# A fused attention and two feed-forward blocks: the position bias as one fp32 product per group, the second block on f16 pairs

## Chip, cores, metric

One core of a Trainium2 chip runs the whole kernel in one launch. The metric is the device time of one execution in microseconds. The kernel before took 663.27 us as the median of 3 runs (662.59 to 666.99).

## What is computed

For 2 batches of 8 heads, 576 positions and 64 features, the reference forms attention scores `0.125 * q k^T` and adds a position bias from a small network:

```
x    = log1p(|i - j|) / log1p(max(i, 1))
h    = max(x * w1 + b1, 0)          # 32 units
bias = h @ w2                       # 8 heads
```

A softmax over j follows, a product with v, then a first feed-forward block on 1152 tokens of 512 features (2048 hidden units, a rational function P(h)/Q(h) as activation), and a second one of the same size with `max(0.01 h, h)`. The weights of both blocks arrive as 64-bit floats. The result has to be good to about fp32, so every large product is split into a leading and a trailing part and made as three products: lead*lead, lead*trail, trail*lead.

## The kernel before, in words

The program is written out by hand, engine by engine, in this order.

**Bias stage.** The 576 query rows are handled in 36 groups of 16 rows (`NG`), four rows beside each other in four slots, each slot with 32 partitions for the 32 units. For each slot `b_mask` writes a 0/1 (VectorE) or sign (ScalarE) mask in f16: is the unit on for this distance? `MASKS` says which engine makes which of the four. `b_mm` makes two sums from these masks on TensorE, with f16 coefficients in two parts: per group 2 x 16 products, each with 32 output columns in one of the four column strips of the array. `b_t0` (ScalarE) scales the first sum by a row's factor, `b_t1` (GpSimd) multiplies by the table `te` of log distances, `b_out` (VectorE) adds the second sum, and a DMA on SP's queue puts the 128 x 576 result into the bias tiles. `BIAS_PLAN` says how many groups ahead each step is issued; `EXTRA` mixes in the loads and preparations of the first attention unit.

**Attention.** Eight units (a pair of heads, a batch) of nine tiles each: scores in three fp32r products (`qk`), bias added and minimum taken on VectorE (`ttr`), exp on ScalarE, split into f16 pairs, transposed by DMA, product with v in f16 (`av`). Then `xhi`/`xlo` split the result for the first block. `TAIL` and `START` mix in the beginning of the first block.

**First block.** 16 slices f of 128 hidden units. `w_load` fetches two halves of weights, `w_dve` turns 64-bit floats into fp32 on VectorE in three steps, `w_hi`/`w_lo` split them into fp32r pairs (ScalarE, GpSimd). `gemm1` makes 36 products of 384 columns a slice, the `r_...` steps compute the activation, `split_hi`/`split_lo` split it, `g2_mm` makes the second product over blocks of slices and `g2_acc` adds it up in SBUF. The order is that of a list scheduler (`arrange`) over these steps with assumed costs (`COST`) and ranks (`SHIFT`). For slices in `E_DVE`, which the scheduler does not know, `r_q1` is left out and `r_e` runs on VectorE in its place.

**Second block.** The same with `l_001`, `l_max` for the activation. The order is a fixed step plan (`PLAN2`); `g2_tok` makes 48 products of 512 columns a token tile over all slices and adds six blocks up in SBUF (`BLOCKS`). All its products are fp32r, on the same pairs of tiles as in the first block.

Of the kernel before, what the change touches and what calls it, by code (L numbers as in the profile page):

```python
# [26 lines left out]
MASKS = ('AVAA', 'VVAV', 'VVVV', 'VVAA')  # L27
BIAS_PLAN = [(3, 'mask', 2), (-1, 'mm', 1), (5, 'mask', 0), (1, 'mm', 0), (1, 'extra'), (-1, 'out'),
             (1, 't0'), (1, 't1'), (3, 'mask', 1), (3, 'mask', 3)]
O_LAG = (0, 1)  # L30
O_STEP = (3, 0)
G2_LAG = 10
# [8 lines left out]
}  # L41
E_DVE_1 = ()

SHIFT = {'g2_acc': 285.2,
         'g2_mm': 1.9,
         'g2_out': 44.7,
         'gemm1': 50.3,
         'r_abs': 71.3,
         'r_e': -48.0,
         'r_exp': 178.1,  # L50
         'r_fin': 2.1,
         'r_h2': -90.6,
         'r_h3': -51.4,
         'r_ln': -196.5,
         'r_q1': 110.6,
         'r_qa': -99.6,
         'r_qq': 49.4,
         'r_s1': 54.7,
         'r_v': 204.8,
         'split_hi': 156.3,  # L60
         'split_lo': 25.5,
         'w_dve0': 46.3,
         'w_dve1': 282.1,
         'w_dve2': 149.1,
         'w_hi': 297.1,
         'w_lo': 17.0,
         'w_load': -193.4}
SLACK = 0.34


def arrange(tasks, ends, free):
# [18 lines left out]
    rank = {k: way[k] + SHIFT[k[0]] for k in tasks}  # L90
# [3 lines left out]
    while todo:  # L94
# [7 lines left out]
        t, k = max(((t, k) for t, k in best[eng] if t <= first[eng] + SLACK), key=lambda x: rank[x[1]])  # L102
# [7 lines left out]
        for u in users[k]:  # L110
            missing[u] -= 1
            if not missing[u]:
                ready[u] = max(ends.get(x, 0.0) for x in tasks[u][2]) + 0.15
# [4 lines left out]
PLAN2 = [  # L118
    (6, "w_lo", 0),
    (5, "w_hi", 0),  # L120
    (4, "w_dve", 1),
    (5, "w_hi", 1),
    (7, "w_lo", 1),
    (-2, "gemm1", 3),
    (6, "split_hi"),
    (2, "l_max"),
    (4, "w_dve", 2),
    (3, "w_dve", 0),
    (5, "w_load"),
    (-3, "gemm1", 1),  # L130
    (-4, "gemm1", 0),
    (0, "l_001"),
    (-3, "gemm1", 2),
    (7, "split_lo", ()),
]
# [4 lines left out]
NEX = 2  # L140
HI_MERGED = ()
# [3 lines left out]
PAR = 168 + S // 4 + NG + len(MASKS)  # L145
# [41 lines left out]
E_DVE = (0, 1, 2)  # L187
XLO_POOL = False
EXTRA = [(2, 'load', 0), (4, 'load', 1), (22, 'load', 2), (33, 'load', 3), (35, 'v_scale', 1),
         (15, 'prep_ql', 0, 0), (4, 'late_constants'), (32, 'v_sum', 1), (29, 'prep_vd', 0),  # L190
         (20, 'prep_ql', 0, 1), (15, 'v_scale', 0), (11, 'prep_q', 0, 0), (16, 'prep_q', 0, 1),
         (8, 'v_sum', 0), (10, 'prep_k', 0), (28, 'prep_v8', 0)]
# [10 lines left out]
def host_constants():  # L203
# [5 lines left out]
    e = p // H  # L209

    def away(off):
        return np.abs(c[None, :] - S - off[:, None])

    dist = away(4 * g).astype(np.float16)
    tabs = psi[np.minimum(away(4 * e), S - 1)].astype(np.float32)
    first = np.array([first_row(n) for n in range(NG)])
    first_z = (first[:, None] + 16 * np.arange(4)[None, :]).reshape(-1)
    rows_z = psi_i[4 * g[:, None] + first_z[None, :]]
    rows_e = np.float32(1.0) / psi_i[4 * e[:, None] + first[None, :]]
# [3 lines left out]
    picks = np.array([[pat[y] == "A" for pat in MASKS] for y in range(4)]).repeat(32, 0)  # L223
    rows = np.concatenate([rows_z, rows_e, picks], 1).astype(np.float32)
    small = np.concatenate([eye, k == m[None, :]], 1).astype(np.float32)
    return rows, {
        "dist": np.ascontiguousarray(dist),
# [6 lines left out]
def attn_bias_moe_kernel(  # L234
# [8 lines left out]
    dist: bass.AP,  # L243
# [18 lines left out]
    ln15 = const.tile([128, 1], F32, name="ln15")  # L262

# [8 lines left out]
    ys = [pair_slot(2, p) for p in range(NP)]  # L272

# [7 lines left out]
    raw = const.tile([128, 2, DM], F32, name="raw")  # L281
# [5 lines left out]
    for m, t0 in (("1", 0), ("2", NF + 3)):  # L287
        for f in range(NF):
            if m == "2" or f > 2:
                w_pair.setdefault(t0 + f - 3, []).append(("i" + m, f))  # L290
            if m == "2" or f > 0:
                w_pair.setdefault(t0 + f + O_LAG[int(m) - 1] - (f < O_STEP[int(m) - 1]), []).append(("o" + m, f))
# [8 lines left out]
    def w_dve(t, k, x0=0, x1=2):  # L301
# [4 lines left out]
        for x in range(xs.start, xs.stop):  # L306
            assert holds["w64", x] == t
            holds["raw", x] = t
        if not wide:
            if k == 0:  # L310
                V.tensor_copy(raw[:, xs], w64[:, xs])
            return
        w = w64[:, xs].rearrange("p x (n y) -> p x n y", y=2)
        bits = raw[:, xs].bitcast(I32)
# [7 lines left out]

    def w_hi(t, x):
        if x < len(w_pair.get(t, ())):
            m, f = w_pair[t][x]
            ring = wi_ring if m[0] == "i" else wo_ring
            slot = ring[(f + NF * (m[1] == "2")) % len(ring)]
            assert holds["raw", x] == t
            holds[m[0], (f + NF * (m[1] == "2")) % len(ring)] = None
            w_got[m, f] = slot  # L330
            A.activation(w_got[m, f][0], raw[:, x], AF.Copy)  # L331

    def w_lo(t, x):
        if x < len(w_pair.get(t, ())):
            assert holds["raw", x] == t
            m, f = w_pair[t][x]
            holds[m[0], (f + NF * (m[1] == "2")) % len(wi_ring if m[0] == "i" else wo_ring)] = (m, f)
            hi_, lo_ = w_got[m, f]
            G.tensor_tensor(lo_, raw[:, x], hi_.bitcast(F32), ALU.subtract)  # L339

    def weights(m, f):
        ring = wi_ring if m[0] == "i" else wo_ring
        assert holds[m[0], (f + NF * (m[1] == "2")) % len(ring)] == (m, f), (m, f, holds)
        return w_got[m, f]
# [4 lines left out]
    def gemm1(m, f, kk, cs=range(3)):  # L349
        if kk == 0 and 0 in cs:  # L350
            hps[f] = psh[f % 2].tile([128, 3, 512], F32, tag="h", name="ph")
        ps = hps[f]
# [5 lines left out]
        for n, c in todo:  # L358
            w, x = ((hi_, xh), (hi_, xl), (lo_, xh))[n]
# [80 lines left out]
    def l_001(f):  # L440
        s1[f] = t32("s1", 3)
        A.activation(c3(s1[f]), hp(f, None), AF.Copy, scale=0.01)  # L442

    def l_max(f):
        V.tensor_tensor(c3(s1[f]), hp(f, None), c3(s1[f]), ALU.max)
# [6 lines left out]
    def split_lo(f, dve, c=None):  # L452
# [3 lines left out]

    early = {
        f.__name__: f
        for f in (r_abs, r_s1, r_qq, r_qa, r_h2, r_h3, r_ln, r_exp, r_q1, r_e, r_v, r_fin, split_hi, split_lo)
        + (w_load, w_dve, w_hi, w_lo)  # L460
# [67 lines left out]
    with ExitStack() as st:  # L528
# [8 lines left out]
        z = b1p.tile([128, 2 * S], F16, name="z")  # L537
# [4 lines left out]
        A.dma_start(out=z, in_=dist)  # L542
        SP.dma_start(out=te[:, halves[0]], in_=tabs[:, halves[0]])
# [3 lines left out]
        c0, c1 = 134 + S // 4, 134 + S // 4 + NG  # L547
        rows_z, rows_e, picks = pr[:, 134:c0], pr[:, c0:c1], pr[:, c1:]
# [10 lines left out]
        G.memset(ones, 1.0)  # L559
        G.memset(tiny, 1e-30)  # L560
        G.memset(ln15, float(15 * np.log(2)))

        sg, aw, rate = col1("sg"), col1("aw"), col1("rate")
        V.tensor_scalar(sg, wc[:, 0:1], 0.0, 2.0, ALU.is_ge, ALU.mult)
        V.tensor_scalar(sg, sg, -1.0, None, ALU.add)
        V.tensor_scalar(aw, wc[:, 0:1], sg, 1e-30, ALU.mult, ALU.max)
        V.reciprocal(aw, aw)
        V.tensor_tensor(rate, sg, wc[:, 1:2], ALU.mult)
        V.scalar_tensor_tensor(rate, rate, -1.0, aw, ALU.mult, ALU.mult)
        V.tensor_scalar(rate, rate, 13.2, -13.2, ALU.min, ALU.max)  # L570
        nwc = b1p.tile([128, 2], F32, name="nwc")
# [634 lines left out]
```

## Time and profile before

| | |
|---|---|
| median of 3 runs | 663.27 us (662.59 to 666.99) |
| the profiled execution | 666.41 us |
| its span, first to last instruction | 664.6 us |
| mean granted TensorE clock | 0.964 |
| busy: PE / DVE / ACT / POOL | 593.9 / 514.6 / 408.7 / 360.5 us |
| chain that ended last | PE 54%, DVE 18%, DMA 6%, ACT 5%, issue 5% |

PE is TensorE's product row, PEld its weight loads, DVE VectorE, ACT ScalarE, POOL GpSimd, SP the engine whose queue issues DMAs. `L360` is line 360 of the kernel. In a row of the grouped view, after the bar stand the busy time in us, the mean ns of one, and the idle time of that engine just before such instructions with what ended it. Products are pipelined, and their ends are modelled: a row of n products in a row shows n steps and one drain.

### The profile page before, as it was taken

To read this page: it belongs to the slowest core of one execution; us is meant where nothing else is said; L and a number is where in the kernel's file an instruction comes from. 1 tells how busy PE (TensorE), PEld (TensorE's weight loads), DVE (VectorE), ACT (ScalarE), POOL (GpSimd) and SP (SyncE) were. 2 spreads that over 40 slices of the span, in tenths; PEclk is the share of its full clock that TensorE was granted. 3 is DMA by queue.
4 is the path that set the end of the run, shared out by engine and by line. 5 is a ranking of instruction groups with operands and counts; after the bars stand their busy time and mean duration, and the time that the engine had idled before them with its cause. 6 is when DMAs were issued, how large, how long until landed. Compare 5 with 4: busy or idle time off the path is not lost.

```text
span 664.6 us, 11791 instructions
## 1 busy us (share of the span) xinstructions
PE 593.9 (89%) x4595; PEld 527.5 (79%) x4595; DVE 514.6 (77%) x788; ACT 408.7 (61%) x625; POOL 360.5 (54%) x263
## 2 busy tenths in 40 slices
PE   5767878898988857779999999999999999999998
PEld 3334557777777746779999999999999999999876
DVE  7999897979889787998999999997355745545463
ACT  9999678778878467687776786653355322322210
POOL 5766685757776512357567577652265443453340
PEclk9998979988989998879999999999999999999999
DMA  5767889999979912111131130121133221220113
GB/s 188 194 153 208 218 153 194 199 204 193 159 140 167 229 64 95 65 64 64 64 122 70 64 126 33 65 65 63 64 127 126 97 95 63 88 104 32 64 47 127
DMA packets 102199, 77.35 MB, mean 116 GB/s; under 512 B 86400, under 2 KB 86784, under 8 KB 102144
## 3 DMA queue, kind: packets, MB, share of 16 engines
q1 hardware_dynamic: 100848, 68.97, 40.7%
q10 hardware_dynamic: 1296, 7.64, 3.6%
q8 instruction: 36, 0.59, 0.4%
q14 instruction: 19, 0.16, 0.1%
HBM read 42.39 MB, written 2.36 MB: 67 GB/s over the span
## 4 chain that ended last, share of the span: by engine, by line
PE 54%; DVE 18%; DMA 6%; ACT 5%; issue 5%; POOL 2%; SPq 0%; DVEq 0%; POOLq 0%; ACTq 0%
PE ph L360 21%; PE pz L982 13%; PE py L941 11%; PE ps L722 5%; DMA biasr<-in_moe_w_in 3%; DVE raw L319 3%; DVE raw L317 2%; PE pv L814 2%; DVE raw L321 2%; DMA et<-hl 2%; ACT ex L750 1%; DVE pt L734 1%; DMA qkv<-in_qkv 1%; PE pr L841 1%; DVE ph L413 1%
## 5 line engine op out<-in xcount | busy, mean ns | idle before, releaser
L360 PE MATMUL ph<-bias,bias 128*128 128x384 f32 x1152 | 215.9, 341 | 14.6 <-DVE s L434 11.8
L360 PEld LDWEIGHTS ph<-bias,bias 128*128 128x128 f32 x1152 | 206.5, 192 | 20.3 <-ACT bias L951 6.9
L787 POOL TENSOR_TENSOR hl<-ex,hl 128x512 f16<-128x512 f32 (+2 forms) x94 | 92.3, 1000 | 35.2 <-DVE hl L774 18.8
L722 PE MATMUL ps<-kt,qz 128*128 128x288 f32 x432 | 81.0, 331 | 18.8 <-DVE mn L734 14.8
L339 POOL TENSOR_TENSOR wo<-raw,wo 128x512 fp32r<-128x512 f32 x23 | 31.1, 1351 | 116.8 <-ACT wo L331 116.8
L455 POOL TENSOR_TENSOR gl<-s,gh 128x1152 fp32r<-128x1152 f32 (+1 forms) x33 | 84.1, 2548 | 11.5 <-ACT gh L450 11.0
L722 PEld LDWEIGHTS ps<-kt,qz 128*128 128x128 f32 x432 | 65.5, 206 | 30.1 <-DVE mn L734 16.9
L339 POOL TENSOR_TENSOR bias<-raw,bias 128x512 fp32r<-128x512 f32 x37 | 51.1, 1382 | 58.7 <-ACT bias L331 48.5
L941 PE MATMUL py<-gh,wo 128*128 128x384 f32 x288 | 78.7, 337 | 1.7 <-DVE bias L953 1.6
L982 PE MATMUL pz<-wo,gh 128*128 128x512 f32 (+1 forms) x240 | 74.5, 386 | 0.3 <-DVE bias L990 0.3
L990 DVE TENSOR_TENSOR bias<-pz,bias 128x512 f32<-128x512 f32 x40 | 27.6, 690 | 52.9 <-PE pz L982 52.9
L750 ACT ACTIVATE ex<-pt,mn 128x576 f32<-128x576 f32 x72 | 55.2, 767 | 17.6 <-DVE mn L734 13.7
L630 PEld LDWEIGHTS <-coef 128*32 128x32 f16 x1152 | 28.5, 100 | 40.5 <-issue 25.8
L648 POOL TENSOR_TENSOR t<-t,te 128x576 f32<-128x576 f32 x36 | 47.0, 1311 | 22.4 <-DVE bb L653 12.7
L941 PEld LDWEIGHTS py<-gh,wo 128*128 128x128 f32 x288 | 52.5, 188 | 3.7 <-DVE bias L953 3.6
L442 ACT ACTIVATE s<-ph 128x1152 f32<-128x1152 f32 x16 | 18.2, 1136 | 57.9 <-PE ph L360 57.9
L734 DVE CUSTOM_DVE_ANT_0 pt<-ps,bias 128x576 f32<-128x576 f32 x64 | 47.5, 745 | 7.4 <-PE ps L722 5.3
L317 DVE TENSOR_SCALAR raw<-biasr 128x1024 int32<-128x1024 int32 (+1 forms) x40 | 33.6, 841 | 24.0 <-DMA biasr<-in_moe_w_in 22.6
L941 PE MATMUL py<-gl,wo 128*128 128x384 f32 x156 | 52.2, 334 | 0.0
L331 ACT ACTIVATE wo<-raw 128x512 fp32r<-128x512 f32 x27 | 16.9, 628 | 55.9 <-DVE raw L321 55.9
L982 PEld LDWEIGHTS pz<-wo,gh 128*128 128x128 f32 x240 | 44.3, 188 | 7.7 <-DVE bias L990 0.7
L982 PE MATMUL pz<-wo,gl 128*128 128x512 f32 (+1 forms) x129 | 50.1, 389 | 0.0
(134 smaller groups left out, 1185.5 us busy)
## 6 DMA issues: line engine op xcount, KB each, us to landing
biasr<-in_moe_w_in SPq DMA_DIRECT2D x32, 512.0 KB, 4.5
biasr<-in_moe_w_out SPq DMA_DIRECT2D x32, 512.0 KB, 3.6
bias<-bb SPq DMA_DIRECT2D x32, 288.0 KB, 3.9
qkv<-in_qkv ACTq DMA_DIRECT2D x8, 896.0 KB, 5.5
out<-bias SPq DMA_DIRECT2D x8, 256.0 KB, 2.0
biasr<-bb SPq DMA_DIRECT2D x8, 144.0 KB, 3.6
et<-hl SPq DMA_TRANSPOSE x40, 4.8
sm<-in_small SPq DMA_DIRECT2D x1, 416.0 KB, 5.1
```

The lines of the kernel that those rows point to most:

```text
L317: V.tensor_scalar(bits, hi32, 3, 0x3FFFFFF8, ALU.logical_shift_left, ALU.bitwise_and)
L339: G.tensor_tensor(lo_, raw[:, x], hi_.bitcast(F32), ALU.subtract)
L360: PE.matmul(ps[:, c, 0:CH], w[:, sl], x[kk][:, c * CH:(c + 1) * CH], start=(kk == 0 and n == 0), stop=(kk == KD - 1 and n == 2),)
L455: eng.tensor_tensor(part(gl, c), part(s1[f], c), part(gh, c).bitcast(F32), ALU.subtract)
L630: PE.matmul(ps[32 * c:32 * c + 32, lo:hi], coef[:, int(MASKS[n % len(MASKS)][c] == "A"), j, part], masks[n, c][:, lo // 64:hi // 64], star ...
L648: G.tensor_tensor(t1, t0s.pop(n), te[:, S - first_row(n):2 * S - first_row(n)], ALU.mult)
L722: PE.matmul(ps[:, c, 0:288], lt[:, a], kts[i][:, b, 288 * c:288 * c + 288], start=(n == 0), stop=(n == 2),)
L734: V.tensor_tensor_reduce(out=c2(pt), in0=s_ps.pop((i, j))[:, :, 0:288], in1=c2(bsrc), op0=ALU.add, op1=ALU.min, scale=1.0, scalar=3.0e38, ...
L750: A.activation(et, pt, AF.Exp, bias=mn, scale=-1.0, accum_out=sums[i][:, col:col + 1],)
L787: engines[j in at].tensor_tensor(hl[:, xs, dst], e9[:, xs, src], hl[:, xs, src], ALU.subtract)
L941: PE.matmul(ps[:, 0:CH], w[:, sl], gts[f][x][:, cs], start=(f == f0 and m == 0), stop=(f == f0 + nf - 1 and m == 2),)
L982: PE.matmul(ps[:, half], gts[f][x][:, sl], w[:, half], start=(f == f0 and m == 0), stop=(f == f0 + nf - 1 and m == 2),)
```

## The change

Bias: the unit's value itself is made in fp32, `max(slope * te, -b1)` on VectorE or `Relu(slope * te + b1)` on ScalarE, with `slope = w1 / log1p(i)` per row; one fp32 product with w2 per slot and half row sums the units; one ScalarE step negates it, adds a constant for the slots made on VectorE, and is the group's result. The masks, thresholds, coefficient splits, the multiplication by the table on GpSimd and the second sum go.

Second block: weights (per pair of halves) and tokens (per chunk of 384) are scaled by 2^15 over the root of their sum of squares and split into f16 pairs instead of fp32r pairs; products are f16; the scale is taken back when the second product is added up. New steps: `w_sq`, `w_sum`, `w_sig`, `w_lo2` per weight pair, `y_sq`, `x_sum`, `x_sig`, `x_cast`, `x_low`, `x_inv` per token chunk. Both halves of a load are now of one kind (two of w_in or two of w_out). The second product runs in eight blocks of two slices. The scheduler now orders both blocks in one list, with ranks that differ at the ends (`seam`), and there are two `raw` buffers. `E_DVE` is (0,) instead of (0, 1, 2).

```diff
-MASKS = ('AVAA', 'VVAV', 'VVVV', 'VVAA')
+MASKS = ('VAAV', 'AAVV', 'VVVV', 'VVVV')
+OUTS = 'AAAA'
-E_DVE = (0, 1, 2)
+E_DVE = (0,)
+BLOCKS_2 = [2] * 8
...
+    def w_sq(t):
+        if t in w_pair:
...
+                A.activation(junk, raws[max(t, 0) % 2], AF.Square, accum_out=w_ss[t])
+    def total(ss, col):
+        spare = live[-2][:, 0, 384 + col:385 + col]
+        for x in range(ss.shape[-1]):
+            PE.matmul(spare, ones_r, ss[:, x:x + 1], start=(x == 0), stop=(x == ss.shape[-1] - 1))
+        return spare
+    def root_of(dst, spare):
+        A.activation(dst, spare, AF.Ln, bias=tiny)
+        A.activation(dst, dst, AF.Exp, bias=ln15, scale=-0.5)
...
-            G.tensor_tensor(lo_, raw[:, x], hi_.bitcast(F32), ALU.subtract)
+                V.scalar_tensor_tensor(lo_, raws[max(t, 0) % 2][:, x], sig[m, f - f % 2][0], hi_, ALU.mult, ALU.subtract)
...
         def b_mask(n, c):
-            mk = mp.tile([128, 9, 66], F16, tag="mk", name="mk")[:, :, 0:64]
+            mk = mp.tile([128, S], F32, tag="mk", name="mk")
...
-                V.tensor_scalar(mk, zs, thr[:, col:col + 1], None, ALU.is_gt)
+                eng.tensor_scalar(mk, src, slope[:, col], off, ALU.mult, ALU.max)
...
+        def b_mm(n):
+            ps = (psa, psb)[n % 2].tile([128, 1024], F32, tag="AB"[n % 2], name="ps" + "AB"[n % 2])
+            for x in range(2):
+                for c in range(4):
+                    PE.matmul(
+                        ps[32 * c:32 * c + 32, 512 * x:512 * x + 288], wflat, masks[n, c][:, 288 * x:288 * x + 288],
+                        start=True, stop=True,
+                    )
...
-            V.scalar_tensor_tensor(bb, psB.pop(n)[:, 0:S], cab[:, v, 1:2], t1s.pop(n), ALU.add, ALU.add)
+                A.activation(to, ps[:, :, 0:288], AF.Identity, bias=base[:, v:v + 1], scale=-1.0)
...
-                V.tensor_tensor(dst, ps[:, half], dst, ALU.add)
+                V.scalar_tensor_tensor(dst, ps[:, part], back, dst, ALU.mult, ALU.add)
...
+        elif k[0][:4] == "gemm" and k[2] == 0 and (k[0] != "gemm2" or k[1] > 1):
+            for x in list(waiting):
+                ops[x[0]](x[1])
+                del waiting[x]
```

The last lines issue a pair's `w_sig` (which reads the sum from a spare column of the previous slice's PSUM tile) at the latest before the next slice's first product, which writes that tile.

## Rows read from the trace of the kernel before

**Rows 1.** Stretch, length, busy us of PE, PEld, DVE, ACT, POOL; PE clock, DMA share, GB/s.

```profile
0.00:79.00 79.00, 54.97 (x1180) 31.90 (x1180) 72.10 (x150) 71.55 (x109) 51.83 (x50) 0.98 0.68 191
...
245.00:300.00 55.00, 39.24 (x181) 37.72 (x182) 49.59 (x45) 39.36 (x46) 21.09 (x12) 0.81 0.20 69
300.00:460.00 160.00, 158.26 (x905) 156.13 (x904) 150.09 (x180) 111.74 (x128) 99.44 (x51) 1.00 0.21 73
460.00:640.00 180.00, 179.28 (x915) 164.03 (x914) 93.80 (x103) 57.02 (x71) 79.24 (x45) 1.00 0.24 85
```

**Rows 2.** What PE waited for, 245 to 300 us: total, times, longest in us.

```profile
PE ph L360 <- DVE s L434: 11.8, 3, 6.6
```

**Rows 3.** Chain of waits (start, length in us): products of the two blocks.

```profile
300.08 6.24 PE ph L360 x36
...
511.05 2.08 PE pz L982 x9
```

**Rows 4.** Timeline of PE (start, length in us): products in bf16, f16, fp32, fp32r.

```profile
69.16 0.46 PE L504 MATMUL psA<-qkv 128*128 128x128 bf16 x5
...
155.67 1.72 PE L814 MATMUL pv<-et,vs 128*64 128x256 f16 x28
...
172.14 0.39 PE L830 MATMUL pr<-sm,r 128*9 128x128 f32 x2
172.46 1.06 PE L722 MATMUL ps<-kt,qz 128*128 128x288 f32 x6
173.45 0.30 PE L814 MATMUL pv<-et,vs 128*64 128x256 f16 x2
```

**Rows 5.** Timeline: a sum on PE and the ScalarE step that reads it.

```profile
74.49 0.38 PE L514 MATMUL psA<-vsc,ones 128*128 128x1 f32 x2
...
74.91 0.26 ACT L515 ACTIVATE vsc<-psA,tiny 128x1 f32<-128x1 f32 x1 [0.65 <-PE psA L514]
```

**Rows 6.** Grouped instructions, whole span: steps like those that the second block gains.

```profile
L450 ACT ACTIVATE gh<-s 128x1152 fp32r<-128x1152 f32 x30 | 34.7, 1156 | 2.0 <-DVE s L437 1.6
...
L319 DVE SCALAR_TENSOR_TENSOR raw<-biasr,raw 128x512 int32<-128x512 int32 x16 | 14.0, 877 | 0.2
```

**Rows 7.** Grouped VectorE instructions, 245 to 300 us: `r_e` of slices 1 and 2.

```profile
L429 DVE SCALAR_TENSOR_TENSOR qq<-qq,onep,r 128x1152 f32<-128x1152 f32 x2 | 3.4, 1692 | 0.0
```

**Rows 8.** Timeline: first and last bias result, first attention tile.

```profile
11.74 0.82 DVE L653 SCALAR_TENSOR_TENSOR bb<-psB,cab,t 128x576 f32<-128x576 f32 x1 [0.28 <-POOL t L648]
...
77.53 0.82 DVE L653 SCALAR_TENSOR_TENSOR bb<-psB,cab,t 128x576 f32<-128x576 f32 x1 [0.62 <-POOL t L648]
78.90 0.76 DVE L734 CUSTOM_DVE_ANT_0 pt<-ps,bias 128x576 f32<-128x576 f32 x1 [0.55 <-DVE bb L653]
```

**Rows 9.** Grouped instructions of the bias stage, 0 to 79 us, by shape.

```profile
L622 DVE TENSOR_SCALAR mk<-z,thr 128x576 f16<-128x576 f16 x90 | 40.6, 502 | 0.0
L620 ACT ACTIVATE mk<-z,nthr 128x576 f16<-128x576 f16 x54 | 39.5, 769 | 0.0
...
L642 ACT ACTIVATE t<-psA,ca_i,par 128x576 f32<-128x576 f32 x36 | 29.6, 824 | 3.0 <-PE psA L630 1.7 <-POOL t L648 1.2
```

**Rows 10.** Timeline, VectorE: a scalar step with and without a per-partition operand; an fp32 cast.

```profile
5.42 0.29 DVE L592 TENSOR_SCALAR thr<-thr,sg 128x144 f32<-128x144 f32 x1
5.75 0.23 DVE L593 TENSOR_SCALAR nthr<-thr 128x144 f32<-128x144 f32 x1
...
80.65 0.46 DVE L774 CAST hl<-ex 128x576 f16<-128x576 f32 x1 [0.31 <-ACT ex L750]
```

**Rows 11.** Timeline of PE: the mask products, two early pairs, then a round of 16.

```profile
9.70 0.61 PE L630 MATMUL psB<-mk,coef 128*32 128x512 f16 x2
...
12.92 0.38 PE L630 MATMUL psB<-mk,coef 128*32 128x512 f16 x2
...
44.47 0.67 PE L630 MATMUL psB<-mk,coef 128*32 128x512 f16 x16 [0.40 <-DVE bb L653]
44.96 0.40 PE L630 MATMUL psA<-mk,coef 128*32 128x512 f16 x3
```

More of the change, by code (lines that the diff above doesn't have):

```diff
@@ new lines, with seam @@
+SLACK = 0.23
+for task in COST:
+    SHIFT.setdefault(task, 0.0)
+LATE = {"w_sum": 3.0, "w_sig": 0.8, "x_sum": 1.0, "x_sig": 0.8}
+def seam(k):
+    name, n = k[0], k[1]
+    if name[0] in "xy" or name == "gemm0":
+        return str(n)
+    if name[:2] in ("r_", "sp") and not name.endswith("2") or name == "gemm1":
+        return "<" if n < 3 else ">" if n > 13 else ""
+    if name[0] == "w":
+        return "<" if n < 2 else ">" if NF <= n < NF + 4 else ""
+    if name[:2] == "g2":
+        return str(n)
+    return "<" if n < 3 else ""
@@ L76, in arrange @@
+def arrange(tasks, ends, free, shift, slack):
     way = {}
@@ L101, in arrange @@
         eng = min(first, key=first.get)
-        t, k = max(((t, k) for t, k in best[eng] if t <= first[eng] + SLACK), key=lambda x: rank[x[1]])
+        t, k = max(((t, k) for t, k in best[eng] if t <= first[eng] + slack), key=lambda x: rank[x[1]])
         end = t + tasks[k][3]
@@ L590, in attn_bias_moe_kernel @@
[L590 to L604 removed]
+        slope = b1p.tile([128, S // 4], F32, name="slope")
@@ L1028, in w_tasks @@
             part = len(pair) / 2
-            add(("w_dve0", t), [("w_load", t)] + [(x, t - 1, y) for x in ("w_hi", "w_lo") for y in range(2)], part)
+            add(("w_dve0", t), [("w_load", t)] + [(x, t - 2 + (t == 0), y) for x in ("w_hi", "w_lo", "w_lo2") for y in range(2)], part)
             add(("w_dve1", t), [("w_dve0", t)], part)
             add(("w_dve2", t), [("w_dve1", t)], part)
+            if t >= NF and pair:
+                add(("w_sq", t), [("w_dve2", t)])
+                add(("w_sum", t), [("w_sq", t)])
+                add(("w_sig", t), [("w_sum", t)])
@@ new lines, in plan_all @@
+        last = None
+        for c in range(3):
+            for f in range(2):
+                for kk in range(KD):
+                    key = ("gemm2", f, kk) if c == 2 else ("gemm0", f, kk, c)
+                    add(key, [("x_low", c, kk), made["i2", f], last] + [("r_v", NF - 1, x) for x in range(3)], 1.0 if c < 2 else 0.336)
+                    last = key
+        for f in range(NF):
+            if f > 1:
+                for kk in range(KD):
+                    add(("gemm2", f, kk), [last, made["i2", f], ("l_max", f - 2)])
+                    last = ("gemm2", f, kk)
+            add(("l_001", f), [("gemm2", f, KD - 1), ("split_lo2", f - 3)])
+            add(("l_max", f), [("l_001", f)])
+            if f < G_BUFS:
+                gone = [("g2_mm", *u) for u in u_of[held[NF + f - G_BUFS]]]
+            else:
+                gone = [("t_mm", blocks_of[f - G_BUFS], k) for k in toks]
+            add(("split_hi2", f), [("l_max", f), ("split_hi2", f - 1)] + gone)
+            add(("split_lo2", f), [("split_hi2", f)])
@@ new lines, in plan_all @@
+        pre = before[-4:]
+        for bi, (f0, nf) in enumerate(blocks_2):
+            for k in toks:
+                fs = range(f0, f0 + nf)
+                add(("t_mm", bi, k), [("split_lo2", f) for f in fs] + [made["o2", f] for f in fs] + pre[-2:-1] + pre[-3:-2], nf / 2)
+                acc = "t_acc" if bi else "t_out"
+                add((acc, bi, k), [("t_mm", bi, k)] + ([("x_low", c, k // 2) for c in range(3)] if bi == 0 and k < 8 else []) + [("x_inv", c) for c in range(3)])
+                pre = [("t_mm", bi, k), (acc, bi, k)] if 0 else pre + [("t_mm", bi, k), (acc, bi, k)]
```

605 lines of the change are left out of this document (348 added, 257 removed), and 5 rows, old and new, of the table COST.

## The prediction, made before the kernel was run

> **What bounds the kernel now.** I read the busy time by stage first, because the stages have different limits [rows 1]. In the bias stage VectorE and ScalarE are busy for 72 of 79 us each, PE for 55: two engines hold it together. In the second block (460 to 640) PE is busy for 179.3 of 180 us and VectorE for 94: PE alone. The first block from 300 on is PE (158 of 160) with VectorE close behind (150). In the ramp before it PE idles for 16 of 55 us while VectorE works for 50, and the list of waits says that PE waited 11.8 us there for VectorE's `r_v` [rows 2]. The change leaves attention alone. So I price the bias stage by the slowest of three engines, the second block by PE, the ramp by VectorE.
>
> **Second block, products.** A steady run of 36 products of 384 columns takes 6.24 us, 173 ns each; nine of 512 take 2.08 us, 231 ns [rows 3]: 0.451 ns a column in fp32r. For f16 the nearest row is the product with v: 28 products, two strips side by side, so 14 steps of 256 columns; 1.72 us less the 0.30 of one pair is 13 steps of 0.109 us, 0.426 ns a column, of which some 2 ns a product look fixed (256 columns at 2.4 GHz are 106.7 ns) [rows 4]. (The rest of the 0.30, 0.19, is the drain that every last product shows.) That gives 162 ns for 384 columns and 216 for 512. The block has 16 x 36 = 576 of the first and 9 x 48 = 432 of the second: 576 x 11 ns + 432 x 15 ns = 6.3 + 6.7 = 13.0 us less. Bounds: 0 (f16 in full width no faster than fp32r) and 14.5 (nothing fixed). All of it is on the path, as PE never rests there.
>
> **Second block, the new steps.** Sums on PE: 16 for weights, 3 x 4 for tokens, each one short bf16 product; five bf16 products of 128 columns take 0.46 us, less the drain 0.27, so 0.055 a step [rows 4]; with some slack 28 x 0.06 = 1.7 us more. Each sum makes PE wait in its own order: before it for ScalarE's `w_sq`, and behind it the next slice's first product, with all that is queued after that, waits for the ScalarE step that reads the sum out of the tile which that product writes. From the sum's start to that read's end is 0.68 us when ScalarE is free [rows 5]. There are 19 such places: 0 us if products of the other kind lie between, 13 us if none do. The scheduler orders them; the stretch that it ordered before (300 to 460) left PE 1.7 us of idle [rows 1], so I take 2 and keep both ends.
>
> At the seam a token chunk's chain (square, sum, two short ScalarE steps, cast, remainder) is some 3.4 us: 0.82 + 0.38 + 2 x 0.26 + 0.82 + 0.88 at most [rows 5, 6, 9]. It is covered by the first two chunks' products of slices 0 and 1, 2 x 24 x 0.162 = 7.8 us; were that cover gone, it would cost 3.4. Off the path: VectorE gains 32 weight remainders and 18 additions of at most 0.88, some 44 us on 94 of 180 [rows 1, 6]; ScalarE gains 16 squares of 1.16 and some 50 short steps of at most 0.82, under 60 us on 57. PE's work covers both. Loads, their queue and the output stores stay as many: 64 half loads, now two of a kind, and ten stores on SP. GpSimd loses 32 weight remainders, for which nobody waits in this block.
>
> **Ramp.** `r_e` of slices 1 and 2 leaves VectorE, 3.4 us [rows 7], for GpSimd, and two ScalarE steps come back. GpSimd is busy for 21 of 55 us there, ScalarE for 39 [rows 1], so they have room. VectorE holds the ramp and nearly the block behind it, so the whole 3.4 comes off; the new list and the second `raw` buffer could add some, and VectorE's weight remainders for the second block, made before the seam, could take some back: -6 to +2. I take -3.4.
>
> **Bias stage.** A group took (77.53 - 11.74) / 35 = 1.88 us [rows 8]. Now ScalarE has one unit step and one result per group: 0.77 + 0.82 = 1.59 us by its old mask and its old PSUM step [rows 9]. VectorE has three fp32 unit steps. An fp32 cast of this shape takes 0.46, a per-partition operand adds 0.06 [rows 10], so 0.52 each, 1.56 a group; the upper end is 0.76, an fp32 step with two inputs [rows 8], 2.28 a group, which would cost 11 us more than I forecast. GpSimd is out. PE: an fp32 product is two records in the same columns, and the pair of 128 columns takes 0.39 us, 0.20 without the drain, so 0.10 a record against 0.055 in bf16 [rows 4]: two passes a record. So 288 columns take 0.245 us a record, 0.49 a product, eight products a group. What they cost together no row shows, as no fp32 product here has neighbours in other strips. The f16 masks do: 16 products, 4608 columns, start within 0.49 us, 9.4 columns per ns, so four strips really stream at once [rows 11]. By that the eight cost 0.98 us. With no overlap they cost 3.92. Between them: strip 0's first record starts, its second must wait for the same strip, and strip 1's records stand behind it in PE's queue. If starts keep to program order, one product begins every 0.245 us and a group costs 1.96. The f16 rows never put two records of one strip ahead of another strip, so they can't tell. I take 1.96: it follows from two things, the pair of records that the rows do show and a single queue.
>
> The Trainium skill says the same of the queue (PSUM — Partial Sum Buffer, Engine vs sequencer instructions: matmuls start and complete in program order); by that the group costs 1.96 us.
>
> Then PE holds the stage: 36 x 1.96 = 70.6 us. To this come a start at about 6 us (the first result now, at 11.74 [rows 8], has three engines' steps and about 6 us behind it; an estimate), 2.5 us because PE runs at about half speed until 12 us (the same pair with its drain takes 0.61 before and 0.38 after [rows 11]), and 1.7 us for the four sums for v (0.46 and 0.38, twice [rows 4, 5]): PE is done at 80.8. The first attention tile needs its scores first, 1.1 to 1.3 us [rows 4]: 82.1 instead of 78.90 [rows 8]. With a little idling I take +4.
>
> **The sum.** -13.0 + 1.7 + 2 - 3.4 + 4 = -8.7 us. The profiled execution took 666.41 us, so 657.7 on its scale. It lay 3.1 above the median; on the median's 663.27 the sum gives 654.6, and I forecast 655. A change of less than 1%, 6.6 us, can't be told from none here.
>
> **Rivals.** *Strips side by side.* If PE overlaps four fp32 products as it does f16 ones, it needs 1 us a group, and ScalarE at 1.59 holds the stage. ScalarE's 71.6 us lose 18 masks, 13.8, and 1.5 of old preparation [rows 1, 9]; VectorE needs 1.56 a group. The stage ends some 11 us earlier than now instead of 4 later: 655 - 15 = 640. For it speaks the f16 row; against it, that a strip's two records follow each other.
>
> The Trainium skill gives this rival its rule (TensorE: Matmul & The Clock Gate, Measured speedup vs the span model): three products in 32-column strips ran 2.38 times as fast as one after the other, and each further strip adds about 4 ns to the span. By it the eight products take about 1 us. No run here shows it for fp32.
>
> *Strips one after another (slower).* If fp32 keeps strips from overlapping, a group costs 3.92 us, 36 x 1.96 = 70.6 more: 655 + 70 = 725. Its place is PE in the bias stage; it decides from 2.2 us a group (0.28 a product), where 36 groups have eaten the 8.7 us. Against it speaks that f16 strips overlap in the same array.
>
> *Sums hold PE.* All 19 reads stand bare on PE's path: +11 over the forecast, 666. For it: the forced order ahead of a slice's first product. Against it: token products to put between.
>
> *f16 is no faster.* Full-width f16 costs what fp32r does, and the change does not do what it says: 655 + 13 = 668. Against it stands the 0.426 ns a column.
>
> **Chances.** Forecast 0.47 (655, its own range 648 to 662 by the bounds of ramp, seam and sums), side by side 0.32 (640, give or take 5), one after another 0.06, sums hold PE 0.10, f16 no faster 0.05. The range of 636 to 667 holds nearly all of the first two and half of the small middle ones; left out are 725 and the upper part of the two near 667. Faster by over 1% means below 656.6: three fifths of the forecast and nearly all of side by side, 0.60. Slower by over 1%, above 669.9: 0.06, half of f16 no faster, a third of the sums, 0.12. Within 1%: 0.28.
>
> **What would show it.** In the bias stage PE's row at 9 tenths or more, starts 0.245 us apart and ScalarE and VectorE with idle time say forecast; starts of four strips a few ns apart and ScalarE full say the first rival; 0.49 apart the second. In the second block nine products should take 1.46 and 1.94 us instead of 1.58 and 2.08, with PE idle for under 1 part in 20; idle on PE ended by the step that reads a sum says sums hold PE. In the ramp PE's wait for `r_v` should fall to about 8 us. A first attention tile before 70 us or after 90 would make the forecast wrong, as would PE idle of over 6 us in the second block.

## The result, and the profile after

The changed kernel takes 645.52 us (median of 4 runs, 643.80 to 651.51), against 665.13 us for the kernel before in the same session (662.59 to 669.77). The ratio is 0.969, 95% interval 0.965 to 0.973. The profiled execution took 646.13 us with a span of 644.3 us, 20.3 us less than the span before. I had forecast 655 us: the direction held, the size did not, and the range held only because it was drawn around a rival as well (the forecast's own range was 648 to 662). One run of e8 below (1113.75 us, at a granted clock of 0.557 where all others have 0.95 or more) is left out of its median and ratio.

From the two traces, in us (each stretch ends where the next begins):

| stretch | before | after | difference | forecast |
|---|---|---|---|---|
| start to first attention tile | 78.9 | 65.3 | -13.6 | +4 |
| to the last product with v | 152.9 | 155.0 | +2.1 | 0 |
| to the first block's last product | 227.8 | 226.8 | -1.0 | -3.4 |
| to PE's last instruction | 202.0 | 193.9 | -8.1 | -9.3 |

The busy time by stage of the kernel after, with the columns of [rows 1]; the stretches are the same stages, now earlier:

```profile
0.00:65.00 65.00, 54.12 (x599) 23.86 (x600) 57.55 (x120) 58.75 (x86) 20.23 (x11) 1.00 0.80 225
233.50:288.50 55.00, 41.48 (x196) 39.66 (x197) 45.40 (x44) 43.32 (x51) 28.31 (x14) 0.84 0.19 68
288.50:447.00 158.50, 156.79 (x896) 152.59 (x895) 150.59 (x173) 116.99 (x149) 93.78 (x48) 1.00 0.23 84
447.00:641.00 194.00, 188.53 (x1034) 99.61 (x1033) 158.74 (x191) 90.03 (x143) 39.00 (x16) 1.00 0.22 81
```

In the first row VectorE (57.55) and ScalarE (58.75) are busy for most of the 65 us. PE's 54.12 holds the drains of many short rows; its 36 groups make 35 of them by the 0.98 us a group that is read below. In the last, VectorE works for 159 of 194 us, where it had 94 of 180 before: it took on weight remainders and scaled additions.

The bias stage's instructions, grouped (0 to 65 us), beside [rows 9]:

```profile
L765 DVE TENSOR_SCALAR mk<-te,slope,off 128x576 f32<-128x576 f32 x108 | 53.6, 575 | 0.0
L772 PE MATMUL psB<-mk,hd 128*32 128x288 f32 x288 | 36.0, 426 | 4.0 <-DVE mk L765 3.9
...
L762 ACT ACTIVATE mk<-te,hd,slope 128x576 f32<-128x576 f32 x36 | 29.1, 863 | 0.1
...
L783 ACT ACTIVATE bb<-psA,base 128x576 f32<-128x576 f32 x18 | 13.2, 736 | 3.0 <-PE psA L772 1.8 <-ACT mk L762 0.8 <-DMA bias<-bb 0.2
L783 ACT ACTIVATE bb<-psB,base 128x576 f32<-128x576 f32 x18 | 13.2, 732 | 1.1 <-DMA bias<-bb 0.6 <-ACT bb L783 0.3 <-PE psB L772 0.2
```

108 units on VectorE take 53.6 us, 0.50 each where I had 0.52; no VectorE idle time stands before them. PE's idle time is ended mostly by VectorE's units (tile `mk`; 3.9 us in the row shown), not the reverse. The first attention tile follows at 65.27 instead of 78.90 [rows 8]:

```profile
65.27 0.76 DVE L864 CUSTOM_DVE_ANT_0 pt<-ps,bias 128x576 f32<-128x576 f32 x1 [2.45 <-PE ps L852]
```

How the fp32 products start can be read from windows of a few tens of ns (PE's records in or across each, in brackets, then clock, DMA share, GB/s):

```profile
33.28:33.32 0.04, 0.03 (x4) 1.00 1.16 461
33.32:33.54 0.22, 0.22 (x4) 1.00 0.83 314
33.54:33.59 0.05, 0.05 (x8) 1.00 0.41 139
```

Four records begin within 40 ns, none in the next 220 ns, then the next four (the eight are four that drain and four new). In single records: 33.290, .296, .303, .310, then 33.556, .563, .570, .576. I read them as one record of each strip per round: four strips run side by side, a round takes about 0.245 us, and a group's 16 records 0.98 us.

The second block's products, from the chain of waits, against [rows 3]:

```profile
500.15 1.46 PE ph L528 x9
...
504.40 1.29 PE pz L1140 x6
```

Nine of 384 columns take 1.46 us and nine of 512 would take 1.94 by the row of six, to the digit what I had. What PE waited for from the ramp to the end:

```profile
PE ph L528 <- DVE s L602: 9.5, 2, 5.1
...
PE ph L455 <- DVE s L613: 1.8, 1, 1.8
PE pz L1140 <- DVE bias L1159: 1.5, 3, 1.1
PE ph L528 <- ACT w L489: 1.4, 1, 1.4
...
PE ph L528 <- ACT ysig L463: 0.4, 1, 0.4
...
PE ph L528 <- ACT sigs L463: 0.3, 1, 0.3
```

The first row is the ramp's wait for `r_v`, 11.8 before [rows 2]. The others are the second block's 5.4 us: a sum behind VectorE's activation, the additions on VectorE, leading parts of weights on ScalarE, and the scales. That block had 1.0 before.

### The profile page after: what moved, and what is told of

Its sections match the earlier page's. It is cut to its first block, busy times and chain, and to the rows that moved or that the text cites. A ratio compares the mean times of both kernels' runs of the same rounds, so it can differ in the third digit from the quotient of the medians.

```text
span 644.3 us, 10671 instructions
## 1 busy us (share of the span) xinstructions
PE 582.4 (90%) x4044; PEld 436.9 (68%) x4044; DVE 555.6 (86%) x825; ACT 437.3 (68%) x698; POOL 289.1 (45%) x194
## 4 chain that ended last, share of the span: by engine, by line
PE 53%; DVE 23%; ACT 15%; issue 6%; DMA 3%; DVEq 0%; SPq 0%; ACTq 0%; POOL 0%
PE ph L528 18%; PE pz L1140 14%; PE py L1078 10%; PE ps L852 4%; DVE mk L765 4%; ACT ex L880 2%; DVE s L605 2%; PE pv L944 2%; DMA et<-hl 2%; DVE pt L864 2%; DVE raw L441 2%; ACT ah L564 2%; DVE raw L443 2%; ACT s L568 2%; PE psA L772 1%
## 5 line engine op out<-in xcount | busy, mean ns | idle before, releaser
L528 PE MATMUL ph<-bias,bias 128*128 128x384 f32 x576 | 108.1, 345 | 11.7 <-DVE s L602 9.5
L528 PEld LDWEIGHTS ph<-bias,bias 128*128 128x128 f32 x576 | 104.0, 195 | 14.0 <-issue 10.3
L528 PE MATMUL ph<-x,w 128*128 128x384 f16 x576 | 102.0, 326 | 2.1 <-ACT w L489 1.4
L1140 PE MATMUL pz<-w,g 128*128 128x512 f16 (+1 forms) x438 | 101.4, 376 | 1.5 <-DVE bias L1159 1.5
L528 PEld LDWEIGHTS <-w 128*128 128x128 f16 x576 | 55.3, 98 | 45.4 <-issue 4.9
L1140 PEld LDWEIGHTS <-g 128*128 128x128 f16 x438 | 42.7, 98 | 47.2 <-issue 2.0
L1159 DVE SCALAR_TENSOR_TENSOR bias<-pz,inv,bias 128x512 f32<-128x512 f32 x56 | 41.8, 748 | 24.3 <-PE pz L1140 21.3
L765 DVE TENSOR_SCALAR mk<-te,slope,off 128x576 f32<-128x576 f32 x108 | 53.6, 575 | 0.0
L623 POOL TENSOR_TENSOR gl<-s,gh 128x1152 fp32r<-128x1152 f32 (+1 forms) x17 | 41.6, 2455 | 9.0 <-ACT gh L618 8.8
L441 DVE SCALAR_TENSOR_TENSOR raw<-biasr,raw 128x1024 int32<-128x1024 int32 (+1 forms) x36 | 44.9, 1248 | 0.7
L443 DVE SCALAR_TENSOR_TENSOR raw<-biasr,raw 128x1024 int32<-128x1024 int32 (+1 forms) x36 | 41.8, 1160 | 0.9
```

The source lines that it names most:

```text
L441: V.scalar_tensor_tensor(bits, hi32, -0x40000000, bits, ALU.bitwise_and, ALU.bitwise_or)
L443: V.scalar_tensor_tensor(bits, lo32, 29, bits, ALU.logical_shift_right, ALU.bitwise_or)
L528: PE.matmul(ps[:, c, 0:CH], w[:, sl], x[kk][:, c * CH:(c + 1) * CH], start=(kk == 0 and n == 0), stop=(kk == KD - 1 and n == 2),)
L623: eng.tensor_tensor(part(gl, c), part(s1[f], c), part(gh, c).bitcast(F32), ALU.subtract)
L765: eng.tensor_scalar(mk, src, slope[:, col], off, ALU.mult, ALU.max)
L1140: PE.matmul(ps[:, part], gts[f][x][:, sl], w[:, part], start=(f == f0 and m == 0), stop=(f == f0 + nf - 1 and m == 2),)
```

## The experiments

Medians in us; the ratio is to the kernel before, run beside them. The last four columns are the stretches of the table above, in the profiled execution.

| | median | ratio, 95% interval | bias | attention | first block | second block |
|---|---|---|---|---|---|---|
| after | 645.52 | 0.969 (0.965 to 0.973) | 65.3 | 155.0 | 226.8 | 193.9 |
| e1 old bias | 658.33 | 0.988 (0.983 to 0.992) | 79.3 | 152.8 | 227.5 | 193.9 |
| e5 bias alone | 653.84 | 0.982 (0.978 to 0.985) | 65.2 | 158.9 | 227.5 | 201.8 |
| e2 strip rows | 645.27 | 0.968 (0.964 to 0.973) | 65.2 | 152.7 | 227.0 | 193.9 |
| e3 twice | 662.08 | 0.993 (0.991 to 0.996) | 82.4 | 153.0 | 227.2 | 193.9 |
| e8 twice rows | 741.30 | 1.113 (1.109 to 1.118) | 160.7 | 156.1 | 230.0 | 193.9 |
| e9 thrice rows | 673.99 | 1.012 (1.007 to 1.016) | 90.8 | 157.1 | 227.3 | 193.9 |
| e10 fewer units | 643.99 | 0.968 (0.963 to 0.973) | 64.4 | 152.9 | 227.3 | 193.9 |
| e6 unit on GpSimd | 650.08 | 0.974 (0.970 to 0.978) | 68.5 | 151.7 | 227.0 | 193.9 |
| e4 no sums | 642.93 | 0.965 (0.960 to 0.969) | 65.2 | 159.1 | 227.2 | 191.1 |
| e7 `r_e` on VectorE | 648.35 | 0.974 (0.971 to 0.977) | 65.2 | 150.2 | 228.5 | 193.9 |
| e12 split on VectorE | 647.07 | 0.972 (0.969 to 0.975) | 65.4 | 156.6 | 227.1 | 193.4 |
| e11 first block in f16 | 642.07 | 0.964 (0.960 to 0.969) | 65.1 | 156.2 | 222.8 | 193.8 |

Attention, which no version edits, took 150.2 to 159.1 us. So the +2.1 of the changed kernel is scatter, and a single total is read better by its stages.

**e1 and e5, the parts alone.** e1 puts the old bias stage (constants, masks, sums, `b_t0`, `b_t1`, `b_out`, `EXTRA`) into the changed kernel; e5 puts the new one into the kernel before.

> The changed kernel with the bias stage of before in it (f16 masks, two sums, GpSimd's multiplication); the second block and the ramp stay changed. Theory (the bias stage carries most of the gain, 13.6 us by the first attention tile): 645.5 + 11 to 14 = 657 to 660, 0.989 of before, and the first attention tile returns to 78 to 80 us. Rival (the bias stage only starts attention earlier, and attention, which took 2.1 us longer after the change, or a better ordered second block gives the result): 648 to 652. By my forecast's own sum, in which the new bias stage costs 4 us and all else gives 12.7, this would be 652.4.

> The kernel before with the new bias stage alone (fp32 units, one product, one ScalarE step); both feed-forward blocks are those of before. Theory (the stage ends 13 to 14 us earlier, and what follows is as long as before): 665 - 12 to 14 = 651 to 654, 0.980 of before, first attention tile at 65 to 66 us. Rival (part of the gain comes only together with the new second block, for instance by the state in which the queues and buffers reach it): 655 to 660. By the forecast's term for this stage, +4: 669.

By e1 everything but the bias is worth 8.3 us (658.33 against 666.59); by e5 the bias alone is worth 12.8 (653.84 against 666.67). Together 21.1 us, 3.2%, close to the whole change's ratio of 0.969. The parts add up, and the bias stage carries the larger one.

**e2, another order of the strips.**

```diff
-            for x in range(2):
-                for c in range(4):
+            for c in range(4):
+                for x in range(2):
```

> The eight fp32 products of a group in another order: both halves of strip 0, then both of strip 1, and so on, so that four records of one strip stand in a row in the program. Theory (each strip works off its own records and waits for nobody in another strip): the group still takes 0.98 us on PE, first attention tile at 65 to 66 us, 645 to 647 in all. Rival A (starts keep to program order, and the order of the changed kernel only happened to suit it): a strip's four records of 0.245 us hold up the next strip, 13 steps of 0.245 = 3.2 us a group, 36 x (3.2 - 1.5) = 61 us more, 706. Rival B (PE can look past a record that waits for its strip, but only a few records far): records of two or three strips run beside each other, 1.2 to 2 us a group, 0 to 18 us more, 646 to 664.

No change, though four records of a strip now stand ahead of the next strip's first in the program. Windows of one group, PE's records behind the first bracket:

```profile
33.21:33.27 0.06, 0.06 (x5) 0.04 (x5) 0.06 (x2) 0.06 (x1) 0.06 (x1) 1.00 0.85 230
33.27:33.48 0.21, 0.21 (x5) 0.12 (x6) 0.21 (x1) 0.21 (x1) 0.21 (x1) 1.00 1.13 258
33.48:33.54 0.06, 0.06 (x7) 0.04 (x3) 0.06 (x1) 0.06 (x1) 0.06 (x1) 1.00 0.73 154
```

Five records run in the first window, two of them of strip 0 and three new; none is new in the second; three are new in the third. In single records, strips 1 to 3 begin at 33.227, .241 and .258 us, and their second records come at .494, .508 and .525 (strip 0, whose unit was ready sooner, began at 32.467). Strip 2 starts 0.25 us ahead of a record that the program puts before it: program order over the strips does not hold starts back here. The trace does not name a record's strip; I infer it from the four chains of records, 0.24 to 0.27 us apart within a chain.

**e3, e9 and e8, more records.** e3 issues every product twice, in rounds of four strips; e9 issues six records of a strip one behind the other, e8 eight.

```diff
-            for x in range(2):
-                for c in range(4):
+            for x in (0, 1, 0, 1):          # e3
+                for c in range(4):
...
+            for c in range(4):
+                for x in (0, 1, 0):         # e9; in e8 (0, 1, 0, 1)
```

> Every fp32 product of the bias stage is issued twice, the second writing the same sums again: PE's work in the stage doubles to 32 records a group. Theory (four strips side by side, VectorE and ScalarE hold the stage at about 1.5 us a group): PE needs 1.96 us a group, the price that my forecast took for the plain kernel; PE becomes the bound, 36 x 1.96 = 70.6 us and a start of about 10, first attention tile at 81 to 83, 645.5 + 16 = 660 to 664. Rival (more than four records run beside each other, or PE has more slack than its row says): under 5 us more, 646 to 650.

> As with the products issued twice in strip order, but with six records of a strip one behind the other (first half, second half, first half again). Theory (each strip takes in four records, one running and three that wait; while a fifth finds its strip full, nothing behind it starts): the next strip's first record starts when this one's third does, 0.49 us later; a group takes 4 x 0.49 = 1.96 us, PE holds the stage, first attention tile at 81 to 85, 660 to 665. Rival A (six still fit, and only eight were too many): 24 records side by side are 1.47 us a group, no more than VectorE needs: 645 to 649. Rival B (PE looks past three waiting records over all strips together): with four in a row that bound would have shown already, so here it gives no less than 2.9 us a group, 695 or more.

> Each fp32 product issued twice, and the eight records of a strip one behind the other in the program. Theory (each strip works off its own records; PE looks past at least eight that wait for their strip): 1.96 us a group, as with the round-robin order: 660 to 664. Rival (PE looks past only about four records that wait, which the single products in this order never exceeded): the four strips no longer all run beside each other, 2.5 to 5 us a group, 680 to 770.

Timeline of PE in e3: groups of 32 records, 1.94 us apart.

```profile
37.33 2.12 PE L772 MATMUL psA<-mk,hd 128*32 128x288 f32 x32
39.27 2.12 PE L772 MATMUL psB<-mk,hd 128*32 128x288 f32 x32
```

This is the load that my forecast gave the plain kernel, and it gives the forecast's stage: first attention tile at 82.4 us, where I had 82.1. The rest of that sum held as a whole; the price of the products did not. Timeline of PE in e8, where psA and psB alternate by group:

```profile
38.18 0.43 PE L772 MATMUL psB<-mk,hd 128*32 128x288 f32 x1
38.41 0.41 PE L772 MATMUL psA<-mk,hd 128*32 128x288 f32 x1
...
38.66 0.41 PE L772 MATMUL psA<-mk,hd 128*32 128x288 f32 x1
...
38.90 0.41 PE L772 MATMUL psA<-mk,hd 128*32 128x288 f32 x1
...
42.18 0.43 PE L772 MATMUL psA<-mk,hd 128*32 128x288 f32 x1
```

The new group's first record (psB, 38.18) starts while three records of the group before it (psA) still wait for their strip; the next group begins 4.00 us later, so a strip begins every 1.00 us, with its predecessor's fifth record. In e9 a strip begins with its predecessor's third record of six, again when three are left:

```profile
38.26 2.46 PE L772 MATMUL psB<-mk,hd 128*32 128x288 f32 x20
40.32 0.43 PE L772 MATMUL psA<-mk,hd 128*32 128x288 f32 x1
...
42.38 0.43 PE L772 MATMUL psB<-mk,hd 128*32 128x288 f32 x1
```

2.06 us a group, 0.515 a strip. In e2, with four in a row, three are left as soon as the first has started, and nothing is held. All three fit one reading: a strip takes one running record and three that wait, and only when it is full does what stands behind it wait. As every product here is two records, they fit one running product and one that waits just as well; no run tells records from products. The theory stated for e8 fell; that for e9 had the mechanism and missed the total by 9 us, of which 3.6 are 0.025 us a strip, 144 times. Besides, the four groups in which sums for v stand take 3.4 to 3.5 us in e9, where e3's take 2.4 to 2.9, and attention took 157.1 us. What lies behind the limit of four was not tried.

**e10, fewer units on VectorE.** In every third and fourth group slot 2 takes slot 3's values.

```diff
         def b_mask(n, c):
+            if n % 4 > 1 and c == 2:
+                masks[n, c] = masks[n, 3]
+                return
```

> 18 of VectorE's 108 unit steps are left out (in every third and fourth group slot 2 uses slot 3's values, so the bias is wrong there): 8.8 us less for VectorE. Theory (VectorE and ScalarE hold the bias stage together, ScalarE being busy for 58.8 us of its 65): it ends only 1 to 4 us earlier, first attention tile at 61 to 64, 641 to 644. Rival A (VectorE alone holds it): 8 to 9 us earlier, 637. Rival B (PE or the stores of the bias hold it): no change, 645.

8.8 us less on VectorE end the products at 59.3 us instead of 64.0, but bring the first tile forward by 0.9 us only, a little less than the theory had; in the total this can't be told from rival B's "no change". The timeline of ScalarE shows what is next:

```profile
60.34 0.74 ACT L786 ACTIVATE bb<-psB,base 128x576 f32<-128x576 f32 x1 [0.54 <-DMA bias<-bb]
61.58 0.74 ACT L786 ACTIVATE bb<-psA,base 128x576 f32<-128x576 f32 x1 [0.50 <-DMA bias<-bb]
62.83 0.74 ACT L786 ACTIVATE bb<-psB,base 128x576 f32<-128x576 f32 x1 [0.51 <-DMA bias<-bb]
```

Results follow 1.24 us apart and each waits for a buffer whose store has not ended. So behind VectorE (3 units, 1.49 us a group by the busy time of the grouped rows) and ScalarE (a unit and a result, 1.54) seem to stand the stores with about 1.24, read from the four last results alone, and only then PE with 0.98.

**e6, units on GpSimd.** `MASKS` gets one `G` in its third pattern.

> One unit step of every fourth group goes from VectorE to GpSimd, which has nothing else to do in the stage: 9 of 108. Theory (VectorE's fp32 unit steps, one behind the other, keep GpSimd out: its step for the keys of the first unit of attention lasted 17.6 us after the change and 1.43 before): each such unit comes late, the group's product waits, VectorE runs out of mask buffers, only then GpSimd gets in; per unit 1.4 us or more against the 0.49 that VectorE saves: 650 to 660, with GpSimd steps of over 5 us in the trace. Rival (GpSimd works beside VectorE and the 17.6 us had another cause): VectorE's 53 us of units fall by 4.4 and the stage by 2 to 4: 641 to 643, GpSimd steps of 1.0 to 1.5 us.

Slower by 4.6 us by the medians (the intervals just overlap), and by 3.2 us at the first tile. Timeline of GpSimd:

```profile
30.05 13.37 POOL L765 TENSOR_SCALAR mk<-te,slope,off 128x576 f32<-128x576 f32 x2 [4.60 <-PE psB L772]
46.17 3.81 POOL L765 TENSOR_SCALAR mk<-te,slope,off 128x576 f32<-128x576 f32 x1 [2.76 <-PE psB L772]
51.68 3.69 POOL L765 TENSOR_SCALAR mk<-te,slope,off 128x576 f32<-128x576 f32 x1 [1.70 <-PE psB L772]
```

A unit that VectorE makes in 0.49 us takes GpSimd 2.3 to 10.6 beside it (the first row's two are 10.56 and 2.81). A step that takes 2.3 us once and 10.6 another time is held up, but no run shows what GpSimd would need with VectorE idle: how much of this is the engine's own speed stays open.

**e4, without the sums.** Scales are constants; the sums and the steps that read them go.

```diff
-            w_ss[t] = total(w_ss[t], t)
+            pass
...
-            root_of(sig[m, f][0], w_ss.pop(t))
...
+        G.memset(sigs[:, :, 0], 2.0 ** 11)
```

> The second block without the sums on PE and without the two short ScalarE steps that read each of them (the scales are constants instead; the squares stay): what the norms cost on PE's path. Theory (28 steps on PE at 0.03 to 0.06 us are about 1 us, the two waits behind a read are 0.7, and about half of the 3.2 us of idle at the seam comes from weights that wait for their norm): 642 to 644. Rival (VectorE is full at the seam whatever the norms do, so PE's idle only moves): 644.5 to 645.5. My forecast had 3.7 us for the sums and the waits for them: by it 641.8.

The second block is 2.8 us shorter, 191.1 (the medians lie 2.6 apart, with overlapping intervals). What PE still waits for there:

```profile
PE pz L1142 <- DVE bias L1161: 1.5, 3, 1.1
PE ph L527 <- DVE w L500: 1.0, 1, 1.0
PE ph L527 <- DVE s L612: 0.9, 1, 0.9
```

So 2.0 of the 5.4 us of idle and 0.8 of PE's own time belong to the norms; the remaining 3.4 are VectorE's (additions, weight remainders, activation).

**e7, `r_e` of slices 1 and 2 back on VectorE** (`E_DVE = (0, 1, 2)`).

> The changed kernel with `r_e` of slices 1 and 2 on VectorE again, as before the change (and `r_q1` left out for them). Theory (the ramp is not held by VectorE's sum of work but by the order in which slice 0's chain comes back to PE, so these two steps cost little): 645 to 647, ratio to before 0.969 to 0.972. Rival (my forecast's step: VectorE holds the ramp, and 2 x 1.69 us on it all reach the end): 648.5 to 649.5, 0.974.

PE's waits from the ramp on:

```profile
PE ph L528 <- DVE s L602: 11.6, 2, 6.9
```

11.6, close to the 11.8 before the change. The wait moves by 2.1 us for 3.4 us of VectorE's work, and the stretch by 1.0 to 1.7 (228.5 against 226.8 to 227.5 in the runs up to the first block that differ in nothing else there). Of those runs e8 is an exception: with nothing edited in the ramp its wait is 12.5 us and its stretch 230.0. The medians are 2.8 apart, with overlapping intervals. The stretch lies between theory and rival, the total of 648.35 just below the rival's 648.5; with e8's scatter, the price of the step is not shown.

**e12, the split on VectorE.**

```diff
-        G.tensor_tensor(gl, s1[f], gh, ALU.subtract)
+        (V if f < 2 else G).tensor_tensor(gl, s1[f], gh, ALU.subtract)
```

> The trailing parts of the second block's first two activations are made on VectorE instead of GpSimd. In the changed kernel GpSimd makes them at 463.5 to 468.8 us, and two remainders of weights on VectorE take 4.39 us there instead of 1.42. Theory (VectorE waits until GpSimd's step has ended, and this wait stands behind PE's idle of 1.8 us at 470.7): the remainders take 1.4 to 1.5 us again, VectorE pays 2 x 1.3 us itself, PE's idle there falls to 0 to 1: 643.5 to 645.5. Rival (the 4.39 us have another cause, such as the load that fills the same tiles): the remainders stay at 3 us or more, VectorE loses 2.6 us at the seam: 646 to 648.

VectorE's weight remainders at the seam, after and then in e12:

```profile
464.94 4.39 DVE L501 SCALAR_TENSOR_TENSOR w<-raw,sigs,w 128x512 f16<-128x512 f32 x2
```

```profile
468.17 1.40 DVE L501 SCALAR_TENSOR_TENSOR w<-raw,sigs,w 128x512 f16<-128x512 f32 x2
```

The same pair takes 1.40 us once GpSimd is silent. In the changed kernel 29 of the 32 remainders take 0.72 to 0.75 us, and the three that run beside GpSimd's `split_lo2` 1.61, 2.86 and 2.86, each ending 0.55 us after it; the third case, which e12 leaves on GpSimd, is 2.86 there too. So the 4.39 were GpSimd's step, and the rival's load was not the cause. The two subtractions now cost VectorE 1.35 and 1.33, and the block gains 0.5. The theory's total failed all the same: PE's wait at the seam fell only from 1.8 to 1.4, and 647.07 lies in the rival's range (the interval overlaps the changed kernel's).

**e11, the first block in f16 too, without scales.**

```diff
-    xh = [pair_slot(0, p).bitcast(F32R) for p in range(NP)]
+    xh = [pair_slot(0, p).bitcast(F16)[:, 0:2 * S] for p in range(NP)]
...
-            gts[f] = tuple(pools["g"].tile([128, NT], F32R, tag=x, name=x) for x in ("gh", "gl"))
+            gts[f] = tuple(pools["g"].tile([128, 2 * NT], F16, tag=x, name=x)[:, 0:NT] for x in ("gh", "gl"))
```

> The changed kernel with the first block's operands (tokens, weights, activations) also as f16 pairs, without scales, so fit only for inputs whose trailing halves stay in f16's range; its 1152 products of 384 columns become f16. By the 11 ns that a product gained in the second block, PE needs 12.7 us less there. Theory (from 300 to 420 us VectorE is busy for 115 of 120 us in the first block, so it becomes the bound after a third to a half of that): 4 to 8 us less, 638 to 642. Rival A (PE's whole gain arrives): 632 to 634. Rival B (VectorE holds it already, or the order fitted to the old times loses what is gained): 644 to 648.

Busy time from 300 to 420 us, after and then in e11:

```profile
300.00:420.00 120.00, 119.63 (x678) 116.84 (x677) 115.34 (x126) 90.88 (x97) 78.12 (x40) 1.00 0.21 75
```

```profile
300.00:420.00 120.00, 114.19 (x690) 66.97 (x689) 116.13 (x129) 91.17 (x98) 72.15 (x41) 1.00 0.21 75
```

PE goes from full to 114 of 120 while VectorE stays at 116; between 290 and 425 us PE now waits 4.7 us for VectorE's additions, in ten places. Of the 12.7 us that 1,152 times 11 ns make, the stretch gives 4.0 (226.8 to 222.8). The ratio of 0.964 has an interval that overlaps the changed kernel's, so in the total the gain is not shown; in the stage it is. No version here beats the changed kernel by more than can be told, and e11 asks more of its inputs.

## Why the prediction was wrong, step by step

**The bias stage's term failed**: +4 forecast, -13.6 measured, 17.6 us apart. The step was: "strip 0's first record starts, its second must wait for the same strip, and strip 1's records stand behind it in PE's queue", hence 1.96 us a group. Its first half is right: a strip's records follow each other at 0.245 us. The second half is not: up to three waiting records of a strip hold back nobody (e2), and four strips run side by side at 0.98 us a group. e3 shows that the rest of the working held, by giving PE about those 1.96 us: 82.4 against 82.1.

The Trainium skill (PSUM — Partial Sum Buffer, Engine vs sequencer instructions) says that matmuls start in program order. The single records of e2 contradict that across column strips: a first record starts 0.25 us ahead of one that the program puts before it. Only with six and eight records a strip in a row (e9, e8) does the order bind, not with four (e2).

**The rival that came true** was strips side by side, 640 us, and its signs were the ones I had named: four starts a few ns apart, ScalarE nearly full (58.75 of 65 us). A first attention tile before 70 us, which I had set down as speaking against the forecast, came as well. The stage ended 2.6 us earlier than that rival had it (13.6 against 11), and it is VectorE with ScalarE, not ScalarE alone; e10 points to a third limit, the stores, close behind. Its total was 5.5 us too low, as it took over my other terms: -12.7 together, -7.0 in the trace, of which +2.1 are attention's scatter. The Trainium skill gave this rival its rule (TensorE: Matmul & The Clock Gate, Measured speedup vs the span model): a few ns for each further strip. The 7 ns between starts here agree in kind with its 4.

**Second block's products**: right. The steps are 162 and 216 ns, as inferred from the product with v. (The upper bound of 14.5 us was summed wrongly: with nothing fixed, which is 160 and 213.3 ns by the prediction's own 106.7 for 256 columns, it is 15.4.)

**Sums and waits for them**: 3.7 forecast, 2.8 by e4. What I left out is VectorE: "PE's work covers both" holds for the mean, but at the seam, 460 to 480 us, VectorE is busy for 19.9 of 20 us and PE waits for it, and again at the last block's additions. From the end of the first block on, VectorE's busy time rose by 55 us (103.4 to 158.6), where I had some 44. With that, the block gave 8.1 instead of 9.3.

**Ramp**: I took 3.4 because VectorE "holds the ramp". The `r_v` wait fell by 2.3, to 9.5 where I had about 8. The stretch shows only 1.0 of it. In return PE waits 6.4 us for ScalarE's `gh` there, where it waited 5.1. Nine more records of PE now lie in the stretch (1,134 against 1,125 after the last product with v, by count), but they are not the reason: e4 has 1,125 again and takes 227.2. The other runs with the changed ramp take 226.8 to 227.5 (e8 230.0), the kernel before 227.8 and e5 227.5, so a gain of 1.0 can hardly be told from scatter, and neither can the step's price in e7. The step that failed is "the whole 3.4 comes off"; what else sets this wait stays open.

**Attention**: forecast unchanged, and it is, within its own scatter.

## What to carry to other kernels

Before taking a queue as strict, look for a row in which an instruction starts ahead of one that blocks, and if the trace has none, let both prices stand with near equal chances; here 0.47 against 0.32 was too sure. fp32 products in column strips, as here, cost the same in both orders that were tried as long as no more than four records (two products) of one strip stood in a row. When two engines hold a stage together, look for the third limit (here, it seems, the stores, at 1.24 us a group) before pricing the next edit.

## What the runs showed of the hardware that was not expected

GpSimd and VectorE can hold each other up for whole instructions. GpSimd's step for the keys, 1.43 us in the kernel before, took 17.6 after the change:

```profile
20.92 17.60 POOL L673 TENSOR_TENSOR kt<-qkv,kt 128x576 fp32r<-128x576 f32 x1 [17.65 <-ACT kt L672]
```

VectorE runs 0.49 us units without a pause through most of that time, and GpSimd's step ends at 38.52 us, beside a `qz` step of VectorE. The same step took 10.8 us in e9 and 8.1 in e10. A VectorE without pauses is not the whole condition, though. In e3 the step took 1.44:

```profile
25.02 1.44 POOL L673 TENSOR_TENSOR kt<-qkv,kt 128x576 fp32r<-128x576 f32 x1 [21.75 <-ACT kt L672]
21.66 9.53 DVE L765 TENSOR_SCALAR mk<-te,slope,off 128x576 f32<-128x576 f32 x17
```

VectorE's 17 units stand as close there, and it is one of them that was held, for 1.69 us. In e6 the step took 1.42. What decides who goes first stays open.

The other way round, the weight remainders of e12's section took 4.39 us instead of 1.40 while GpSimd made `split_lo2`. Not every VectorE step is held: the activation `l_max` at 463.68 us, which reads one input from PSUM, takes its usual 1.35 us beside the same GpSimd step. The Trainium skill (SBUF — State Buffer, SBUF: two separate sides) states an exclusive lock on a port pair that the two engines share, held for the whole instruction; of VectorE's steps it names those in a two-port mode and those with two inputs in SBUF. The remainders (two inputs in SBUF, held) and `l_max` (one, not held) agree. That the losing engine can be passed over by some 30 short instructions in a row is what the 17.6 us add. Here nobody waited for the keys; had the first scores needed them earlier, it would have been the bound of the stage.
